# A recurrent attention block and its gated layer on one core: sums of squares by one-column products, an engine chosen per unit, and dummy products

## The chip, the cores and the metric

The kernel runs on one NeuronCore of a Trainium2 chip. The metric is device time in microseconds (us) of one execution: 171.41 us, the median of three runs (170.92 to 173.13).

The core's engines work side by side, each through its own queue in order: TensorE (PE, matrix products; its weight loads, PEld, are a row of their own), VectorE (DVE), ScalarE (ACT), GpSimd (POOL) and SyncE (SP), which in this kernel issues all transfers. SBUF is the working memory, PSUM the memory that products are written to.

## The reference

Four batches of eight heads, 768 steps, head size 48. The first half is a recurrence with a decaying 48x48 state for each head, the second a layer of 384 to 1024 to 384 with a softmax gate and a normalization.

```python
for t in range(S):
    cur = einsum('bhd,bhe->bhde', u * k[t], v[t])
    y[:, :, t] = einsum('bhd,bhde->bhe', r[t], state + cur)
    state = w[t][..., None] * state + einsum('bhd,bhe->bhde', k[t], v[t])
x = y as (B * S, H * D)
h = x @ w_in
e = exp(h - max(h));  solu = h * e / sum(e)
ln = (solu - mean(solu)) / sqrt(var(solu) + 1e-6) * g_ln
out = ln @ w_out
```

All inputs and the output are float32.

## The kernel before, in words

The steps are cut into six chunks of 128 and the batches taken one by one, which makes 24 units (chunk, batch), chunk outermost. A unit's 128 rows pass through some thirty short stages, each a function of its own (lines 213 to 449). The names in the table below, such as `Y7`, are a stage and a unit.

The attention half of a unit: `load` (L110) brings w, k, r and v, 192 KB each. `lw` is the logarithm of w (ACT). `cum` sums it over the chunk by two products with triangular matrices, 384 columns each, and `exp` (ACT) turns the sums into decays in place. `kp` and `rp` (DVE) scale k and r by them, `krk` and `krr` transpose them on PE (four products each, into the PSUM tile `kr_ps`), `kr` (DVE) copies the result out, `M` multiplies them to eight 128x128 score matrices, `m` (ACT) copies those out and `sel` (POOL) sets the part on and below the diagonal of each to zero. The bonus of the current step is `p` = r k, `q` = p u (POOL), `dg` its sum over a head (DVE) and `dv` = v dg (POOL). `Y` (L307) adds on PE, into one PSUM tile `y_ps`: `dv` by a product with the identity, the part from the state, and scores times v (`vb`, v in bf16). `y` (ACT) copies it out. `S`, `et` and `st` (L330 to 371) make the next state: `S` adds the old state (product with the identity), four one-column products that sum the logarithms over the chunk, and k times v; `et` takes the exponential of that sum, `st` multiplies by it in two halves of 64 partitions (DVE).

The layer half: `X` transposes y (PE), `xT` copies it out (DVE), `H` (L388) makes h by 24 products of 128 columns into `h_ps`, `e` (ACT) its exponential, `he` (DVE) h times e. `Oa` and `Ob` (L407) walk over eight slices f of 128 hidden values, four each. For each f there are three products with weights of its own: `he` times the second layer's weights `w2` and a column that gives the mean (385 columns into `o_ps`); `he` times itself, the Gram matrix (128 columns into `g_ps`), of which only the diagonal, the sum of squares, is used; and `e` times a constant column (one column). `junk` (DVE) takes the diagonal, `sq` (ACT), `qm` (POOL) and `lv` (ACT, a logarithm and an exponential) make the scale of each row, and `o` (ACT) scales the output and issues its store.

Once, at the start, `w2` must be built: `gw` scales the eight slices of w_out by the gain (four on DVE, four on ACT), `mean` averages them on PE, `mean_sb` copies that out (ACT), and `w2` (L208) adds it to each slice in eight additions on DVE, in the code's tile names `w`. The first `Oa` needs `w2`. All helpers issue through `InOrder` (L49), which is why most rows of the profile have line 63.

The order of work is a table, `ORDER` (L21): each engine takes its part of the words in the order in which they stand. A load is issued with the word `lw`, four units ahead of it. PSUM is taken from two pools: `big`, two tiles of two banks (`cum`, `M`, `H`), and `small`, four tiles of one bank (the rest). The inputs have six buffers.

## Time and profile before

| | |
|---|---|
| runs | 171.41 us median, 170.92 to 173.13 |
| profiled execution, its own time | 169.39 us |
| its span, first to last instruction | 167.7 us |
| busy PE / DVE / ACT / POOL | 143.0 / 121.2 / 118.0 / 107.5 us |
| bytes moved | 27.09 MB |

A group row of the profile reads: line, engine, operation, what it writes and from what, shape, how often; then busy time in us and the mean of one in ns; then how long the engine idled just before it and for whom. Mean times of neighbours on an engine overlap a little, so that the sum over an engine's groups is larger than its busy time. A row of the timeline begins with its start and its length in us. How fast PE goes is read from the distance between starts, not from the length, since products overlap in its pipeline. The row PEclk of the page, the granted clock, shows nearly full speed throughout.

### The profile page before, as it was taken

What the parts mean: (1) busy time and instruction counts of PE and PEld (TensorE: products, weight loads), DVE (VectorE), ACT (ScalarE), POOL (GpSimd) and SP (SyncE); (2) the same over time, 40 slices, a digit from 0 to 9 for tenths busy, and PEclk for the clock granted to TensorE, in tenths of its full rate; (3) what the DMA queues carried; (4) which work ended last, traced back from release to release, by engine and by line L of the source; (5) the groups of instructions that cost most, each with busy time, mean ns of one, the idle gap of its engine ahead of it and who ended that gap; (6) DMA issues with size and microseconds to landing.
All of it is one profiled execution on the core that took longest, in us unless ns stands there. A gap on an engine that the chain in (4) does not pass through costs nothing.

```text
span 167.7 us, 5377 instructions
## 1 busy us (share of the span) xinstructions
PE 143.0 (85%) x2139; PEld 113.4 (68%) x2139; DVE 121.2 (72%) x280; ACT 118.0 (70%) x243; POOL 107.5 (64%) x157
## 2 busy tenths in 40 slices
PE   0503669928999999999999999999999999999980
PEld 0102336825888888878888778788877878798850
DVE  7008597898978788778988866888677988664430
ACT  3305495618879878788789868987798786767752
...
GB/s 76 224 344 216 348 210 212 170 216 221 177 218 183 218 161 254 188 238 163 240 184 182 266 165 144 185 192 184 192 2 51 0 51 47 51 2 52 92 51 92
DMA packets 104795, 27.09 MB, mean 162 GB/s; under 512 B 100281, under 2 KB 104386, under 8 KB 104770
## 3 DMA queue, kind: packets, MB, share of 16 engines
...
q14 instruction: 9, 0.07, 0.1%
...
## 4 chain that ended last, share of the span: by engine, by line
PE 75%; SPq 8%; DMA 5%; DVE 4%; ACT 2%; POOL 2%; issue 1%; POOLq 0%; DVEq 0%; ACTq 0%
PE o_ps L63 21%; PE h_ps L63 18%; SPq L63 8%; PE y_ps L63 6%; PE g_ps L63 6%; PE kr_ps L63 6%; PE s_ps L63 5%; PE m_ps L63 4%; PE cum_ps L63 4%; DMA wout_f<-in_moe_w_out_dram 3%; DVE w L63 3%; PE x_ps L63 3%; DMA k_in<-in_k_dram 2%; PE mean_ps L63 1%; DVE kr L63 1%
## 5 line engine op out<-in xcount | busy, mean ns | idle before, releaser
L63 PE MATMUL o_ps<-w,he 128*128 128x385 bf16 x192 | 50.7, 325 | 3.4 <-DVE he L63 3.4
L63 PE MATMUL g_ps<-he 128*128 128x128 bf16 x192 | 41.8, 218 | 0.0
L63 POOL TENSOR_SCALAR_AFFINE_SELECT m<-m 128x1024 bf16<-128x1024 bf16 x24 | 26.3, 1096 | 18.3 <-ACT m L63 13.9
L63 PE MATMUL h_ps<-xT,win_sb 128*128 128x128 bf16 x576 | 35.9, 219 | 0.0
L63 PEld LDWEIGHTS <-win_sb 128*128 128x128 bf16 x576 | 32.8, 98 | 0.9 <-DVE xT L63 0.5
L63 PE MATMUL o_ps<-inv_col,e 128*128 128x1 bf16 x192 | 31.9, 166 | 0.0
L63 ACT ACTIVATE e<-h_ps 128x1024 bf16<-128x1024 f32 x24 | 24.5, 1022 | 9.9 <-PE h_ps L63 9.8
L63 DVE TENSOR_TENSOR he<-h_ps,e 128x1024 bf16<-128x1024 f32 x24 | 29.3, 1222 | 2.2 <-ACT e L63 1.3
L63 ACT CAST m<-m_ps 128x1024 bf16<-128x1024 f32 x24 | 24.3, 1012 | 8.5 <-PE m_ps L63 8.2
L63 PEld LDWEIGHTS <-he 128*128 128x128 bf16 x384 | 24.2, 97 | 5.3 <-DVE he L63 3.5
L63 PEld LDWEIGHTS <-e 128*128 128x128 bf16 x192 | 18.5, 96 | 12.8
L63 POOL TENSOR_TENSOR dv<-vb,dg 128x384 bf16<-128x384 bf16 x24 | 19.8, 828 | 9.7 <-DVE dg L63 9.6
L63 POOL TENSOR_TENSOR q<-p,u_bc 128x384 bf16<-128x384 bf16 x24 | 21.8, 911 | 4.6 <-DVE gr L63 4.2
L63 POOL TENSOR_TENSOR p<-r_in,k_in 128x384 bf16<-128x384 f32 x24 | 24.3, 1012 | 0.1
L63 DVE COPY kr<-kr_ps 128x1024 bf16<-128x1024 bf16 x24 | 16.6, 690 | 10.0 <-PE kr_ps L63 9.8
L63 ACT ACTIVATE cum_ps<-cum_ps 128x768 f32<-128x768 f32 x24 | 19.2, 801 | 5.4 <-PE cum_ps L63 3.0
L63 ACT ACTIVATE lw<-w_in 128x384 bf16<-128x384 f32 x23 | 12.0, 522 | 6.7 <-DMA w_in<-in_w_dram 6.7
L63 DVE TENSOR_TENSOR kp<-cum_ps,k_in 128x384 bf16<-128x384 f32 x24 | 13.3, 555 | 3.4 <-ACT cum_ps L63 2.8
L63 PEld LDWEIGHTS <-kr 64*128 64x128 bf16 (+1 forms) x272 | 11.3, 98 | 6.3 <-DVE kr L63 2.8
L63 POOL TENSOR_TENSOR qm<-ss,sq 128x1 f32<-128x1 f32 x24 | 4.5, 190 | 16.9 <-DVE junk L63 13.7
L63 DVE TENSOR_TENSOR st<-s_ps,et 64x192 bf16<-64x192 f32 x40 | 14.1, 353 | 1.6 <-ACT et L63 0.6
L63 ACT ACTIVATE o<-o_ps,rs 128x384 f32<-128x384 f32 x24 | 13.9, 578 | 0.3
...
## 6 DMA issues: line engine op xcount, KB each, us to landing
w_in<-in_w_dram SPq DMA_DIRECT2D x24, 192.0 KB, 4.2
k_in<-in_k_dram SPq DMA_DIRECT2D x24, 192.0 KB, 3.7
r_in<-in_r_dram SPq DMA_DIRECT2D x24, 192.0 KB, 3.9
v_in<-in_v_dram SPq DMA_DIRECT2D x24, 192.0 KB, 4.2
out_dram<-o SPq DMA_DIRECT2D x24, 192.0 KB, 2.7
...
u_row<-in_u_dram SPq DMA_DIRECT2D x1, 1.5 KB
```

Of the source, the lines that this page charges most:

```text
L63: made = make(*args, **kwargs)
```

## The change

The sum of squares no longer comes from the Gram matrix. `hq` squares `he` on ACT or DVE, and `Ob` ends with eight one-column products of `hq` with a column of ones, which write beside the mean in `o_ps`; `g_ps` is gone. `qm` now copies the three sums out and makes the variance in two small instructions, all on DVE; `sq` and `junk` are gone. The four one-column products of the logarithms move from `S` into `cum`, so that `exp` takes the state's decay too; `et` becomes a small multiplication on DVE, and `st` one multiplication over 128 partitions.

The table now names an engine behind a word: `a` ACT, `v` DVE, `g` POOL. So `kr`, `xT`, `m`, `y`, `o`, `hq`, `p`, `q`, `vb`, `dv`, `gw` and the eight additions of `w2` (`wt`) go to different engines in different units. Where `m` is on DVE, one multiplication with the triangular matrix copies and masks, and there is no `sel`. Where `y` is on DVE, it adds `dv` while it copies, and `Y` leaves its product with `dv` out; `Y` with an `x` keeps it. The counts are: `kr` 16 DVE, 8 ACT; `xT` 14 DVE, 10 ACT; `m` 6 DVE, 18 ACT; `y` 14 DVE, 10 ACT; `o` 14 DVE, 10 ACT; `hq` 3 DVE, 21 ACT; `gw` 2 DVE, 3 ACT, 3 POOL; `wt` 4 DVE, 4 POOL; `p` and `vb` one each on DVE, `dv` two, the others POOL. 24 dummy products `dm` of 512 columns on zeros are put in, 19 of them before the first `Oa`, five at the end. The whole order is a new table. The loads of unit 1 now come before the weights, and w_in comes in three pieces.

The diff, cut to its core:

```diff
 ORDER = """
-lw0 cum0 vb0 p0 win1 rows ubc exp0 q0 kp0 p1 rp0 lw1 cum1 dg0 win2 win0 exp1 kp1 krk1 krk0 rp1 krr0 kr0 gw3 M0 dv0 krr1 q1 kr1 m0 dg1 M1 sel0 m1 gw0
...
+dm10 p1g lw0 dm13 dm7 dm12 dm0 p0v dm3 cum0 dm21 exp0 dm20 kp0 et0 krk0 rows rp0 lw1 krr0 cum1 vb0v kr0v M0 ubc exp1 et1 kp1 dm14 m0a q0g krk1 rp1
+sel0 dg0 dv0v krr1 kr1a M1 q1g Y0x win0v y0a dm23 m1v dm5 dm16 win1g X0 win2a gw3a xT0v dg1 H0 vb1g e0 gw2g dv1v Y1 S1 gw0v gw1g y1v gw4a S0 st1 X1
...
+    load(0)
...
-    sp.dma_start(out=win_f, in_=moe_w_in.rearrange("(ko ki) f -> ki ko f", ki=128))
-    load(1)
+    win_v = moe_w_in.rearrange("(ko ki) f -> ki ko f", ki=128)
...
+    load(1)
+    load_w_in(0)
+    load_w_in(1)
+    load_w_in(2)
+    load_w_out(0)
+    load_w_out(1)
+    load(2)
+    for i in range(3, 5):
...
+    own = consts.tile([C, HP, 2], F32)
+    nc.vector.memset(own, 0.0)
+    for a in range(2):
+        nc.vector.memset(own[64 * a:64 * a + 64, :, a:a + 1], 1.0)
+    warm = consts.tile([C, 512], BF16)
+    nc.vector.memset(warm, 0.0)
     inv_col = consts.tile([C, 1], BF16)
-    nc.vector.memset(inv_col, 1.0 / RDF)
...
+    def warm_up(i):
+        w_ps = small.tile([C, 512], F32, tag="s", name="w_ps")
+        pe.matmul(w_ps, lhsT=uti_neg, rhs=warm, start=True, stop=True)
...
-    def setup_w2():
-        for f in range(KF):
-            dve.tensor_add(out=w2[:, f, :DM], in0=gw[:, f, :], in1=mean_sb)
...
+    def setup_w2(f, engine):
+        engine.tensor_add(out=w2[:, f, :DM], in0=gw[:, f, :], in1=mean_sb)
...
     def cumulate(i):
         L = live[i]
         lw = L["lw"]
-        cum = big.tile([C, 2, 512], F32, tag="b", name="cum_ps")
-        pe.matmul(cum[:, 0, :DM], lhsT=uti_neg, rhs=lw[:, :, :D], start=True, stop=True)
-        pe.matmul(cum[:, 1, :DM], lhsT=uts, rhs=lw[:, :, :D], start=True, stop=True)
+        cum = big.tile([C, 1024], F32, tag="b", name="cum_ps")
+        last = units[i][0] == NC - 1
+        pe.matmul(cum[:, 128:512], lhsT=uti_neg, rhs=lw[:, :, :D], start=True, stop=last, skip_group_check=True)
+        pe.matmul(cum[:, 512:896], lhsT=uts, rhs=lw[:, :, :D], start=True, stop=True)
+        if not last:
+            for hp in range(HP):
+                pe.matmul(cum[:, 124 + hp:125 + hp], lhsT=lw[:, 2 * hp:2 * hp + 2, :].rearrange("t a d -> t (a d)"),
+                          rhs=one_col, start=False, stop=(hp == HP - 1), skip_group_check=True)
         L["ex"] = cum
 
     def decays(i):
         cum = live[i]["ex"]
-        act.activation(out=cum[:, :, :DM], in_=cum[:, :, :DM], func=EXP)
+        part = slice(128 if units[i][0] == NC - 1 else 124, 896)
+        act.activation(out=cum[:, part], in_=cum[:, part], func=EXP)
+
+
+    def whole_decay(i):
+        L = live[i]
+        L["et"] = wk.tile([C, HP, 2], F32, tag="et", name="et", bufs=10)
+        dve.tensor_mul(out=L["et"], in0=L["ex"][:, 124:128].unsqueeze(2).to_broadcast([C, HP, 2]), in1=own)
...
-    def transposed_copy(i):
+    def transposed_copy(i, engine):
         L = live[i]
         kr_ps = L["kr_ps"]
         kr = wk.tile([C, 2 * HP, C], BF16, tag="kr", name="kr")
-        dve.tensor_copy(out=kr, in_=kr_ps)
+        copy(engine, kr, kr_ps)
...
-    def scores_copy(i):
+    def scores_copy(i, engine):
         L = live[i]
         m_ps = L["m_ps"]
         m = wk.tile([C, 2, HP, C], BF16, tag="m", name="m")
-        act.copy(out=m, in_=m_ps)
+        if engine is act:
+            act.copy(out=m, in_=m_ps)
+        else:
+            dve.tensor_mul(out=m.rearrange("s a p t -> s (a p) t"), in0=m_ps.rearrange("s a p t -> s (a p) t"),
+                           in1=uts.unsqueeze(1).to_broadcast([C, H, C]))
...
+    def attend(i, with_bonus):
         L = live[i]
         c, b = units[i]
         m, kr, vb, st = L["m"], L["kr"], L["vb"], st_t[b]
         y_ps = small.tile([C, DM], F32, tag="s", name="y_ps")
-        pe.matmul(y_ps, lhsT=ident, rhs=L["dv"].rearrange("t h d -> t (h d)"), start=True, stop=False,
-                         skip_group_check=True)
+        first = True
+        if with_bonus:
+            pe.matmul(y_ps, lhsT=ident, rhs=L["dv"].rearrange("t h d -> t (h d)"), start=True, stop=False,
+                      skip_group_check=True)
+            first = False
         if c > 0:
             for hp in range(HP):
                 pe.matmul(y_ps[:, hp * 2 * D:(hp + 1) * 2 * D], lhsT=kr[:, HP + hp, :], rhs=st[:, hp, :],
-                                 start=False, stop=False, skip_group_check=True)
+                          start=first, stop=False, skip_group_check=True)
+                first = False
         for h in range(H):
             pe.matmul(y_ps[:, h * D:(h + 1) * D], lhsT=m[:, h % 2, h // 2, :], rhs=vb[:, h, :],
-                             start=False, stop=(h == H - 1), skip_group_check=True)
+                      start=first, stop=(h == H - 1), skip_group_check=True)
+            first = False
         L["y_ps"] = y_ps
...
+    def y_copy(i, engine):
         L = live[i]
         y_ps = L["y_ps"]
         y = wk.tile([C, DM], BF16, tag="y", name="y")
-        act.copy(out=y, in_=y_ps)
+        if engine is act:
+            act.copy(out=y, in_=y_ps)
+        else:
+            dve.tensor_add(out=y, in0=y_ps, in1=L["dv"].rearrange("t h d -> t (h d)"))
         L["y"] = y
...
-    def state_decay(i):
-        L = live[i]
-        if units[i][0] == NC - 1:
-            return
-        L["et"] = wk.tile([C, HP], F32, tag="et", name="et")
-        act.activation(out=L["et"], in_=L["s_ps"][:, DM:], func=EXP)
 
     def state_update(i):
         L = live[i]
         c, b = units[i]
         if c == NC - 1:
             return
-        st, s_ps, et = st_t[b], L["s_ps"], L["et"]
-        sv = s_ps[:, :DM].rearrange("p (a e) -> p a e", a=HP)
-        for a in range(2):
-            rows = slice(64 * a, 64 * a + 64)
-            cols = slice(a * D, (a + 1) * D)
-            dve.tensor_mul(out=st[rows, :, cols], in0=sv[rows, :, cols],
-                                 in1=et[rows].unsqueeze(2).to_broadcast([64, HP, D]))
+
+        dve.tensor_mul(out=st_t[b].rearrange("p q (a e) -> p (q a) e", a=2),
+                       in0=L["s_ps"].rearrange("p (h e) -> p h e", h=H),
+                       in1=L["et"].rearrange("p q a -> p (q a)").unsqueeze(2).to_broadcast([C, H, D]))
...
+    def hidden_square(i, engine):
+        L = live[i]
+        L["hq"] = wk.tile([128, KF, C], BF16, tag="hq", name="hq", bufs=3)
+        if engine is act:
+            act.activation(out=L["hq"], in_=L["he"], func=SQUARE)
+        else:
+            dve.tensor_mul(out=L["hq"], in0=L["he"], in1=L["he"])
+
+
     def output(i, part):
         L = live[i]
         e, he = L["e"], L["he"]
         if part == 0:
-            L["o_ps"] = small.tile([C, DM + 2], F32, tag="s", name="o_ps")
-            L["g_ps"] = small.tile([C, C], F32, tag="s", name="g_ps")
-        o_ps, g_ps = L["o_ps"], L["g_ps"]
+            L["o_ps"] = small.tile([C, DM + 3], F32, tag="s", name="o_ps")
+        o_ps = L["o_ps"]
         for f in range(part * KF // 2, (part + 1) * KF // 2):
             pe.matmul(o_ps[:, :DM + 1], lhsT=he[:, f, :], rhs=w2[:, f, :], start=(f == 0), stop=False,
-                             skip_group_check=True)
-            pe.matmul(g_ps, lhsT=he[:, f, :], rhs=he[:, f, :], start=(f == 0), stop=(f == KF - 1))
-            pe.matmul(o_ps[:, DM + 1:], lhsT=e[:, f, :], rhs=inv_col, start=False, stop=(f == KF - 1),
-                             skip_group_check=True)
-
-    def squares(i):
-        L = live[i]
-        junk = wk.tile([C, C], BF16, tag="junk", name="junk")
-        L["ss"] = wk.tile([C, 1], F32, tag="ss", name="ss")
-        dve.scalar_tensor_tensor(out=junk, in0=L["g_ps"], scalar=1.0, in1=ident, op0=MULT, op1=MULT, accum_out=L["ss"])
-
-    def sums(i):
-        L = live[i]
-        L["sq"] = wk.tile([C, 2], F32, tag="sq", name="sq")
-        act.activation(out=L["sq"], in_=L["o_ps"][:, DM:], func=SQUARE)
-
-    def centre(i):
-        L = live[i]
-        L["qm"] = wk.tile([C, 1], F32, tag="qm", name="qm")
-        pool.tensor_sub(out=L["qm"], in0=L["ss"], in1=L["sq"][:, 0:1])
+                      skip_group_check=True)
+            pe.matmul(o_ps[:, DM + 1:DM + 2], lhsT=e[:, f, :], rhs=inv_col, start=False, stop=False,
+                      skip_group_check=True)
+        if part == 1:
+            for f in range(KF):
+                pe.matmul(o_ps[:, DM + 2:], lhsT=L["hq"][:, f, :], rhs=one_col, start=False, stop=(f == KF - 1),
+                          skip_group_check=True)
+
+
+    def variance(i):
+        L = live[i]
+        sums = L["sums"] = wk.tile([C, 3], F32, tag="sums", name="sums")
+        dve.tensor_copy(out=sums, in_=L["o_ps"][:, DM:])
+        neg = wk.tile([C, 1], F32, tag="neg", name="neg")
+        dve.scalar_tensor_tensor(out=neg, in0=sums[:, 0:1], scalar=sums[:, 0:1], in1=sums[:, 2:3], op0=MULT,
+                                 op1=ALU.subtract)
+        L["var"] = wk.tile([C, 1], F32, tag="var", name="var")
+        dve.scalar_tensor_tensor(out=L["var"], in0=sums[:, 1:2], scalar=sums[:, 1:2], in1=neg, op0=MULT,
+                                 op1=ALU.subtract)
...
-        act.activation(out=lv, in_=L["sq"][:, 1:2], func=LN, scale=1e-6 * DF * DF, bias=L["qm"])
+        act.activation(out=lv, in_=L["var"], func=LN)
...
-    def store(i):
+    def store(i, engine):
         L = live[i]
         c, b = units[i]
         o = io.tile([C, DM], F32, tag="o", name="o")
-        act.activation(out=o, in_=L["o_ps"][:, :DM], func=COPY, scale=L["rs"])
+        if engine is act:
+            act.activation(out=o, in_=L["o_ps"][:, :DM], func=COPY, scale=L["rs"])
+        else:
+            dve.tensor_scalar(out=o, in0=L["o_ps"][:, :DM], scalar1=L["rs"], scalar2=None, op0=MULT)
         sp.dma_start(out=out[b * S + c * C:b * S + (c + 1) * C, :], in_=o)
...
+        name, i, choice = re.fullmatch(r"([A-Za-z_]+)(\d*):?([a-z]?)", word).groups()
+        args = [engines[choice]] if choice in engines else []
...
+        if name == "Y":
+            args = [choice == "x"]
+        stages[name](i, *args)
 
```

Three places show how instructions move. The first is PE at the end of a unit's output products (`he`, `e`, `hq` are the weights loaded, `w_192` and `w_204` are the tile `w2`). Before, one of eight rounds:

```order
L63 LDWEIGHTS he
L63 MATMUL o_ps<-w_192,he 128x385
L63 LDWEIGHTS he
L63 MATMUL g_ps<-he 128x128
L63 LDWEIGHTS e
L63 MATMUL o_ps<-inv_col,e 128x1
```

And now, the last of eight rounds and the first of the eight new products behind it:

```order
L67 LDWEIGHTS he
L67 MATMUL o_ps<-w_204,he 128x385
L67 LDWEIGHTS e
L67 MATMUL o_ps<-inv_col,e 128x1
L67 LDWEIGHTS hq
L67 MATMUL o_ps<-one_col,hq 128x1
```

The product of 128 columns has left each round, and eight rows of one column stand behind the eighth.

The second is DVE where `w2` is built and the first h e is made (`he`, unit 0, then unit 1). Before:

```order
L63 TENSOR_TENSOR kp_150<-cum_ps,k_in 128x8x48
L63 TENSOR_TENSOR rp_156<-cum_ps,r_in 128x8x48
L63 TENSOR_TENSOR w_192<-gw,mean_sb 128x384 x8
L63 TENSOR_TENSOR he<-h_ps,e 128x1024
L63 COPY kr<-kr_ps 128x1024
L63 TENSOR_TENSOR st_183<-s_ps,et 64x4x48 x2
```

And now:

```order
L67 TENSOR_TENSOR he<-h_ps,e 128x1024
L67 TENSOR_TENSOR st_195<-s_ps,et 128x384
L67 TENSOR_TENSOR kp_157<-cum_ps,k_in 128x8x48
L67 TENSOR_TENSOR et<-cum_ps,own 128x8
L67 TENSOR_TENSOR rp_165<-cum_ps,r_in 128x8x48
L67 TENSOR_TENSOR w_204<-gw,mean_sb 128x384 x2
L67 TENSOR_REDUCE dg<-q 128x8
L67 TENSOR_TENSOR w_204<-gw,mean_sb 128x384
```

The first `he` now stands ahead of the additions, and DVE makes three of them here and a fourth later; POOL makes the other four.

The third is SP's queue at the start. Before, from the second unit's loads on, with the weights around them:

```order
L63 DMA win_f<-in_moe_w_in_dram 128x3x1024
L63 DMA w_in<-in_w_dram 128x8x48
L63 DMA k_in<-in_k_dram 128x8x48
L63 DMA r_in<-in_r_dram 128x8x48
L63 DMA v_in<-in_v_dram 128x8x48
L63 DMA wout_f<-in_moe_w_out_dram 128x4x384 x2
```

And now:

```order
L67 DMA w_in<-in_w_dram 128x8x48
L67 DMA k_in<-in_k_dram 128x8x48
L67 DMA r_in<-in_r_dram 128x8x48
L67 DMA v_in<-in_v_dram 128x8x48
L67 DMA win_f<-in_moe_w_in_dram 128x1024 x3
L67 DMA wout_f<-in_moe_w_out_dram 128x4x384 x2
```

The weights of the first layer have moved behind unit 1; what follows, the loads of units 2 to 4, stands behind the same bytes as before.

144 lines of the change are left out of this document (72 added, 72 removed).

## The prediction

> **What bounds the kernel now.** I read the busy shares first, then the span in stretches, then the waits, then the timeline of PE.
>
> ```profile
> PE 143.0 (85%) x2139; PEld 113.4 (68%) x2139; DVE 121.2 (72%) x280; ACT 118.0 (70%) x243; POOL 107.5 (64%) x157
> ```
>
> No engine stands out, but the average hides three stages. The stretches are cut at the first and behind the last output product; the columns are length, then busy time of PE, PEld, DVE, ACT and POOL, each with its count, then clock, DMA share and GB/s.
>
> ```profile
> 0.00:30.00 30.00, 14.68 (x116) 8.52 (x117) 16.75 (x58) 13.38 (x21) 14.99 (x28) 1.00 0.93 230
> 30.00:36.50 6.50, 3.17 (x60) 2.93 (x57) 6.34 (x10) 3.04 (x6) 4.24 (x5) 1.00 0.99 195
> 36.50:162.80 126.30, 125.12 (x1967) 102.00 (x1967) 97.84 (x211) 100.31 (x214) 88.06 (x124) 1.00 0.66 147
> 162.80:167.70 4.90, 0.00 (x0) 0.00 (x0) 0.30 (x2) 1.25 (x4) 0.19 (x1) 0.70 0.21 80
> ```
>
> For 126.3 us PE is busy 125.1 while DVE, ACT and POOL have 22, 21 and 30% to spare. So this stretch is PE's work, and a product taken out shortens it. The first 36.5 us are something else: DVE is full from 30 on, and one wait says for what.
>
> ```profile
> 30.16 5.19 DVE L63 TENSOR_TENSOR w<-gw,mean_sb 128x384 bf16<-128x384 bf16 x8 [0.57 <-ACT mean_sb L63]
> 35.27 1.21 DVE L63 TENSOR_TENSOR he<-h_ps,e 128x1024 bf16<-128x1024 f32 x1
> ...
> 36.54 0.34 PE L63 MATMUL o_ps<-w,he 128*128 128x385 bf16 x1 [3.37 <-DVE he L63]
> ```
>
> The eight additions of `w2` hold DVE for 5.2 us, `he` of unit 0 stands behind them, and PE waits 3.4 us for it. The last 4.9 us are the last unit's scale, copy and store.
>
> **PE's work.** What a product costs is the distance to the next start:
>
> ```profile
> 62.62 0.33 PE L63 MATMUL o_ps<-w,he 128*128 128x385 bf16 x1
> 62.78 0.22 PE L63 MATMUL g_ps<-he 128*128 128x128 bf16 x1
> 62.84 0.17 PE L63 MATMUL o_ps<-inv_col,e 128*128 128x1 bf16 x1
> 62.87 0.32 PE L63 MATMUL s_ps<-st,ident 128*128 128x384 bf16 x1
> 63.03 0.24 PE L63 MATMUL s_ps<-one_col,lw 128*128 128x1 bf16 x4
> 63.13 0.33 PE L63 MATMUL s_ps<-vb,kp 128*128 128x96 bf16 x4
> ...
> 65.40 0.33 PE L63 MATMUL y_ps<-dv,ident 128*128 128x384 bf16 x1
> 65.56 0.33 PE L63 MATMUL y_ps<-st,kr 128*128 128x96 bf16 x4
> 65.73 0.36 PE L63 MATMUL y_ps<-vb,m 128*128 128x48 bf16 x8
> 65.93 0.32 PE L63 MATMUL o_ps<-w,he 128*128 128x385 bf16 x1
> ```
>
> A Gram product takes 0.055 us (0.06 as printed), 192 of them 10.6. A one-column product with weights of its own takes 0.025 (four in 0.10 from 63.03); eight narrow ones in a row, each with its own weights, also 0.025 (0.20 from 65.73), so eight weight loads in a row are covered. The 192 new ones cost 192 x 0.026 = 5.0. If their loads were not covered, the price would be that of the Gram products, 10.6, and the swap would bring nothing: the other end. I take 5.0, a gain of **5.6**. The product with `dv`, 0.16, goes in 14 units: **2.2**. The products of the logarithms only move. Together **7.8 us** less for PE, nearly all of it behind the first output product: 126.3 - 7.8 = **118.5**.
>
> **What the others take over.** The nearest rows:
>
> ```profile
> L63 DVE TENSOR_TENSOR he<-h_ps,e 128x1024 bf16<-128x1024 f32 x24 | 29.3, 1222 | 2.2 <-ACT e L63 1.3
> L63 ACT CAST m<-m_ps 128x1024 bf16<-128x1024 f32 x24 | 24.3, 1012 | 8.5 <-PE m_ps L63 8.2
> L63 ACT CAST win_sb<-win_f 128x1024 bf16<-128x1024 f32 x1 | 1.0, 1029 | 0.0
> L63 DVE COPY kr<-kr_ps 128x1024 bf16<-128x1024 bf16 x24 | 16.6, 690 | 10.0 <-PE kr_ps L63 9.8
> L63 DVE TENSOR_TENSOR kp<-cum_ps,k_in 128x384 bf16<-128x384 f32 x24 | 13.3, 555 | 3.4 <-ACT cum_ps L63 2.8
> L63 DVE TENSOR_TENSOR st<-s_ps,et 64x192 bf16<-64x192 f32 x40 | 14.1, 353 | 1.6 <-ACT et L63 0.6
> L63 ACT ACTIVATE o<-o_ps,rs 128x384 f32<-128x384 f32 x24 | 13.9, 578 | 0.3
> L63 ACT CAST y<-y_ps 128x384 bf16<-128x384 f32 x24 | 11.5, 478 | 3.3 <-PE y_ps L63 3.2
> L63 DVE COPY xT<-x_ps 128x384 bf16<-128x384 bf16 x24 | 8.5, 355 | 6.1 <-PE x_ps L63 5.8
> L63 DVE SCALAR_TENSOR_TENSOR junk<-g_ps,ident 128x128 bf16<-128x128 f32 x24 | 6.9, 288 | 8.1 <-PE g_ps L63 4.3 <-PE o_ps L63 3.8
> L63 ACT ACTIVATE sq<-o_ps 128x2 f32<-128x2 f32 x24 | 4.1, 172 | 1.8 <-PE o_ps L63 1.5
> L63 DVE TENSOR_SCALAR gr<-gt_ps 128x8 f32<-128x8 f32 x1 | 0.2, 156 | 0.0
> ```
>
> DVE in the long stretch: 14 `y` and 14 `o` at 0.555 (the `kp` row) +15.5; six `m` at 1.222 +7.3; three `hq` between 0.69 and 1.22, at 0.95, +2.9; 20 `et` at 0.156 +3.1; 20 `st` at 0.555 for 40 at 0.353 -3.0; eight `kr` -5.5; ten `xT` -3.6. The copy of three sums (at most 0.156) and two instructions on one column (between 0 and 0.156 each, say 0.1) stand against `junk`'s 0.288 and its read-out: nothing. Sum +16.7 of row time; neighbours overlap (over all of DVE's groups the means sum to 131 for 121.2 busy), so about nine tenths, **+15**: 97.8 becomes 113, which is 95% of 118.5. ACT: 21 `hq` at 1.029 +21.6, eight `kr` at 1.012 +8.1, ten `xT` at 0.478 +4.8; six `m` -6.1, 14 `y` -6.7, 14 `o` -8.1, 24 `sq` -4.1, 20 `et` at as much as a `sq` -3.4. Sum +6.1, nine tenths +5.5: 100.3 becomes 106, 89%. POOL loses six masks and `qm` and gains little after the start.
>
> So the cover that hid DVE is nearly gone: 28.5 us idle in this stretch before, 5.5 after if PE kept pace. Each queue is in order, and what PE waits for can now stand behind a `y`, an `m` or an `o` of another unit. The added wait lies between 0 (PE keeps pace) and 27 (DVE idles 22.5% as before: 113 / 0.775 = 145.5). In the stretch from 30 to 36.5 DVE was 98% busy, so it can run dense when its operands are there, and `hq` stands several stages of other units' products ahead of the `Ob` that needs it. Behind a late `hq` on ACT wait the next `e` and `m`, and PE's `Ob` and `Y` for those. I take **4**, nearer to the low end.
>
> Transfers do not bind here: 147 GB/s in the long stretch become 147 x 126.3 / 122.5 = 152, and the first 30 us ran at 230. The last 4.9 us keep their length: three small instructions on DVE stand for `junk`, `qm` and `sq`, and the five dummy products at the end have no reader and run beside the last store; should the last store wait for them, five at 0.2 add 1.
>
> **The start.** Of the dummy products, 19 precede the first output product, where PE is busy 17.9 of 36.5 us; at four thirds of 0.16 (512 for 384 columns) they take 4 us, hidden by its idle half; on the path they would cost those 4. In SP's queue unit 1 moves ahead of the weights, past one transfer of 1.5 MB, so that unit 0 and 1 fill PE while the weights land; from unit 2 on nothing arrives sooner. What now decides is the data. The new order puts unit 4's `cum` ahead of the first `Oa`.
>
> ```profile
> 24.66 1.22 SPq L63 DMA_DIRECT2D w_in<-in_w_dram  x1
> ...
> 31.97 0.52 ACT L63 ACTIVATE lw<-w_in 128x384 bf16<-128x384 f32 x1
> ```
>
> ```profile
> w_in<-in_w_dram SPq DMA_DIRECT2D x24, 192.0 KB, 4.2
> ```
>
> Unit 4's w, behind the same bytes as now, is issued at 24.7 and lands 4.2 later, at 28.9; its logarithm takes 0.5, its sums 0.4, `X` 0.2: first `Oa` at 30. On the other side `mean` started at 28.1:
>
> ```profile
> 25.21 0.63 PE L63 MATMUL kr_ps<-ident,kp 128*128 128x128 bf16 x4
> 25.63 0.63 PE L63 MATMUL kr_ps<-ident,rp 128*128 128x128 bf16 x4
> ...
> 28.12 1.48 PE L63 MATMUL mean_ps<-gw,mean_w 128*128 128x384 bf16 x8
> ...
> 32.56 0.38 PE L63 MATMUL kr_ps<-ident,kp 128*128 128x128 bf16 x4
> 32.78 0.39 PE L63 MATMUL kr_ps<-ident,rp 128*128 128x128 bf16 x4
> ```
>
> It now stands earlier on PE, `he` no longer waits for the additions, and half of them go to POOL. I take **30.5** for 36.5, a gain of 6, between 28.9 (w lands) and 36.5 (nothing gained).
>
> The rows also show PE at half rate until about 29: four transposes take 0.42 at 25.21 and 0.22 at 32.56, though the granted clock reads 1.00. The Trainium skill (TensorE: Matmul & The Clock Gate, Part 1) says that PE runs at half clock until it has been busy for about 3.4 us; the trace agrees with the halves, and by that rule the dummies would bring the full rate forward. My sum counts nothing for it, since w of unit 4 decides.
>
> **Sum.** 30.5 + 118.5 + 4 + 4.9 = 157.9 us of span for 167.7. The profiled execution's own time lay 1.7 above its span, which gives 159.6, and 2.0 below the median of the runs. I add half of that: **160.5 us**.
>
> **Rivals.**
> *The order absorbs all.* No added wait, first output at 28.9: 28.9 + 118.5 + 4.9 = 152.3, with 2.7 around it 155. For it: 12 us of slack on ACT. Against it: DVE at 95%.
> *Nothing gained at the start.* The additions interfere:
>
> ```profile
> L63 DVE TENSOR_TENSOR w<-gw,mean_sb x8: 345/668/1155, 30.2 to 35.0; 128x384 bf16<-128x384 bf16 x8
> ```
>
> One took 0.35 to 1.16 us while POOL was at work for most of that time. If DVE and POOL exclude each other there, the split ones come one after the other, four at 0.35 and four at about 0.9 us (POOL's `q` below, of the same size), 5 us, as long as now. First output at 36.5 again: 163.9, with 2.7 around it **166.5**. The Trainium skill (SBUF — State Buffer, Who interferes with whom) says that a DVE instruction with two SBUF inputs and a GpSimd one that reads SBUF lock each other out, which is this case. The spread in the row agrees. Against the rival: the first half of the output needs only four of the eight.
>
> ```profile
> 31.77 0.91 POOL L63 TENSOR_TENSOR q<-p,u_bc 128x384 bf16<-128x384 bf16 x1
> ```
>
> *DVE becomes the bound.* It idles as large a share as before: 30.5 + 145.5 + 4.9 = 180.9, with 2.7 around it **183.5**, slower. It turns when the added wait passes 13.8 us, that is when DVE idles more than 19 us of the stretch. For it: DVE at 95%, in order, with work of five stages more. Against it: DVE's waits before were for PE, which ran dense.
>
> **How the numbers follow.** The forecast 0.54, the order absorbing all 0.20, nothing gained at the start 0.13, DVE as the bound 0.13. Range **151 to 169**: from the second case less 4, to the third and the near half of the fourth. Faster by over 2% (below 168.0; 2% is about what a measurement of this kernel can tell from no change) holds for nearly all of the first three and a little of the fourth, 0.83; within 2% 0.10; slower 0.07.
>
> **What would show it.** Eight `hq` products in about 0.2 us; first `Oa` near 30.5; last output product near 153; DVE over 90% busy between. Wrong if `hq` products take 0.055 each, if the first `Oa` stays at 36, or if PE's waits between come to more than 8 us: then the list of waits names DVE as what they wait for.

## The result and the profile after

The changed kernel takes **161.66 us** (median of four runs, 160.24 to 163.06) against 171.25 for the kernel before on the same chip (four runs, 170.92 to 173.13): a ratio of **0.939**, 95% interval 0.929 to 0.950. Its profiled execution took 161.92 us, with a span of 160.1. Some executions run in a slower state (one of the wide ones below took 230.5 us): medians are over all executions, ratios over those outside that state.

The busy line of the page, then the span in stretches, cut at the first output product, at 112 us, where the last load has just been issued (at 110.7), and behind the last output product. The columns are those of the prediction's table of stretches.

```profile
PE 141.7 (89%) x2147; PEld 109.2 (68%) x2149; DVE 142.9 (89%) x327; ACT 123.4 (77%) x203; POOL 102.5 (64%) x130
```

```profile
0.00:29.10 29.10, 22.31 (x200) 13.46 (x203) 22.91 (x75) 16.86 (x24) 18.05 (x29) 0.82 0.97 240
...
29.10:112.00 82.90, 76.20 (x1258) 61.37 (x1257) 79.46 (x168) 70.22 (x120) 64.42 (x79) 1.00 0.99 208
112.00:155.30 43.30, 41.95 (x690) 33.93 (x689) 38.82 (x81) 35.54 (x58) 20.08 (x24) 1.00 0.17 53
```

The same cut of the kernel before, whose last load is issued at 114.7 us:

```profile
36.50:112.00 75.50, 74.68 (x1186) 61.15 (x1187) 62.46 (x136) 61.56 (x132) 61.35 (x85) 1.00 0.95 199
112.00:162.80 50.80, 50.43 (x784) 40.85 (x780) 35.38 (x76) 38.74 (x83) 26.70 (x40) 1.00 0.24 70
```

Three things are to be seen. The first output product starts at 29.1 instead of 36.5, 7.4 us sooner. From there to the end of the last output product it takes 126.2 us, as long as before: PE's work in it fell from 125.1 to 118.2 us, and its idle time rose from 1.1 to 8.0. And of these 8.0 us, 6.7 lie ahead of 112 us, where the DMA engines are busy 99% of the time and DVE 96%; behind it PE idles 1.4 us of 43. So **the whole net gain was made at the start**, and the 7 us saved in products were given back as waits while loads ran.

The timeline of PE shows the first output product, eight of the new products, and the end:

```profile
29.12 0.33 PE L67 MATMUL o_ps<-w,he 128*128 128x385 bf16 x1
...
33.30 0.34 PE L67 MATMUL o_ps<-one_col,hq 128*128 128x1 bf16 x8
33.50 0.32 PE L67 MATMUL o_ps<-w,he 128*128 128x385 bf16 x1
...
155.12 0.34 PE L67 MATMUL o_ps<-one_col,hq 128*128 128x1 bf16 x8
155.32 0.38 PE L67 MATMUL w_ps<-warm,uti_neg 128*128 128x512 bf16 x1
```

Eight one-column products take 0.20 us, from 33.30 to 33.50. What PE waited for over the whole span (total, times, longest):

```profile
PE kr_ps L67 <- DVE kp L67: 2.2, 3, 1.2
PE w_ps L64 <- POOL uti_neg L152: 1.5, 1, 1.5
PE m_ps L67 <- DVE kr L67: 1.4, 1, 1.4
PE kr_ps L67 <- DVE rp L67: 1.3, 1, 1.3
PE h_ps L67 <- DVE xT L67: 1.2, 2, 0.8
```

The second row and parts of the first and the last belong to the start. The rest are waits for DVE, each short; no single one explains 8 us. Inside the stretch the list has waits of 7.5 us, 6.4 of them for DVE. The groups of DVE show one thing that the prediction had not priced, the two variance instructions on one column:

```profile
L67 DVE SCALAR_TENSOR_TENSOR var<-sums,neg 128x1 f32<-128x1 f32 x24 | 10.6, 441 | 0.8
L67 DVE SCALAR_TENSOR_TENSOR neg<-sums 128x1 f32<-128x1 f32 x24 | 8.8, 367 | 0.8
L67 DVE COPY sums<-o_ps 128x3 f32<-128x3 f32 x24 | 3.6, 152 | 1.8 <-PE o_ps L67 1.7
```

The copy of three columns takes 0.15 us, an instruction on one column two to three times as long. The timeline shows what such a long one stands beside:

```profile
80.23 0.28 DVE L67 SCALAR_TENSOR_TENSOR neg<-sums 128x1 f32<-128x1 f32 x1
...
80.46 0.91 POOL L67 TENSOR_TENSOR q<-p,u_bc 128x384 bf16<-128x384 bf16 x1
80.55 0.84 DVE L67 SCALAR_TENSOR_TENSOR var<-sums,neg 128x1 f32<-128x1 f32 x1
```

`var` started 0.09 us behind POOL's `q` and ended with it. And the list of waits names the loads on POOL and ACT:

```profile
POOL p L67 <- DMA r_in<-in_r_dram: 7.6, 4, 4.7
```

```profile
ACT lw L67 <- DMA w_in<-in_w_dram: 4.2, 5, 1.8
```

This gives the theories. *Lock*: the variance instructions read two operands from SBUF and are shut out while POOL is at work, which costs DVE 9 us. *Loads* (D in the expectations): the transfers hold back the stretch up to 112 us. *PE* (P): PE's products set the time and the waits are incidental. Beside them stands the question which part of the change brought the 7.4 us at the start.

### The profile page after: what moved, and what is told of

It is laid out like the page before. It is cut to its first block, busy times and chain, and to the rows that moved or that the text cites. A ratio compares the mean times of both kernels' runs of the same rounds, so it can differ in the third digit from the quotient of the medians.

```text
span 160.1 us, 5330 instructions
## 1 busy us (share of the span) xinstructions
PE 141.7 (89%) x2147; PEld 109.2 (68%) x2149; DVE 142.9 (89%) x327; ACT 123.4 (77%) x203; POOL 102.5 (64%) x130
## 4 chain that ended last, share of the span: by engine, by line
PE 32%; DVE 31%; SPq 16%; ACT 6%; DMA 6%; issue 6%; DVEq 0%
SPq L67 16%; PE h_ps L67 12%; PE o_ps L67 9%; DVE he L67 7%; DMA w_in<-in_w_dram 5%; DVE neg L67 4%; ACT e L67 3%; DVE var L67 3%; DVE kp L67 3%; PE kr_ps L67 2%; DVE o L67 2%; PE y_ps L67 2%; PE m_ps L67 2%; DVE rp L67 2%; PE s_ps L67 2%
## 5 line engine op out<-in xcount | busy, mean ns | idle before, releaser
L67 PE MATMUL o_ps<-w,he 128*128 128x385 bf16 x192 | 42.7, 325 | 0.5 <-DVE xT L67 0.3
L67 POOL TENSOR_SCALAR_AFFINE_SELECT m<-m 128x1024 bf16<-128x1024 bf16 x18 | 19.6, 1091 | 19.6 <-ACT m L67 19.5
L67 PEld LDWEIGHTS <-he 128*128 128x128 bf16 x192 | 18.5, 97 | 10.7 <-DVE he L67 0.4
L67 ACT ACTIVATE hq<-he 128x1024 bf16<-128x1024 bf16 x21 | 22.1, 1052 | 0.0
L67 ACT ACTIVATE cum_ps<-cum_ps 128x772 f32<-128x772 f32 (+1 forms) x24 | 19.1, 798 | 3.2 <-PE cum_ps L67 2.2
L67 POOL TENSOR_TENSOR dv<-vb,dg 128x384 bf16<-128x384 bf16 x22 | 18.5, 847 | 3.6 <-DVE dg L67 2.6
L67 ACT CAST m<-m_ps 128x1024 bf16<-128x1024 f32 x18 | 18.2, 1010 | 1.2 <-PE m_ps L67 1.0
L67 PEld LDWEIGHTS <-e 128*128 128x128 bf16 x192 | 18.5, 96 | 0.5 <-issue 0.4
L67 PEld LDWEIGHTS <-kp 128*128 128x128 bf16 x176 | 11.2, 98 | 5.5 <-DVE kp L67 3.8
L67 ACT ACTIVATE lv<-var 128x1 f32<-128x1 f32 x24 | 4.9, 203 | 11.4 <-DVE var L67 11.2
L67 PE MATMUL m_ps<-kr 64*128 64x128 bf16 x192 | 10.0, 225 | 4.1 <-DVE kr L67 1.4
L67 DVE TENSOR_REDUCE dg<-q 128x8 f32<-128x384 bf16 x24 | 13.0, 542 | 0.3 <-POOL q L67 0.3
```

The costliest lines, as they stand in the source:

```text
L67: made = make(*args, **kwargs)
```

## The experiments

One table first. "First" is the start of the first output product, "stretch" from there to the end of the last output product (to within 0.2 us), with PE's busy and idle time in it, all from the profiled execution; the ratio is to the kernel before, run beside each on the same chip.

| kernel | median us | ratio, interval | first | stretch | PE busy | PE idle |
|---|---|---|---|---|---|---|
| before | 171.25 | 1 | 36.5 | 126.2 | 125.1 | 1.1 |
| changed | 161.66 | 0.939 (0.929 to 0.950) | 29.1 | 126.2 | 118.2 | 8.0 |
| wide ones | 166.58 | 0.961 (0.951 to 0.972) | 29.8 | 129.6 | 124.1 | 5.5 |
| sums from PSUM | 160.36 | 0.932 (0.924 to 0.940) | 29.4 | 125.1 | 117.2 | 7.9 |
| stores late | 160.64 | 0.933 (0.931 to 0.935) | 29.5 | 125.0 | 117.7 | 7.3 |
| both | **154.63** | **0.899 (0.895 to 0.903)** | 29.9 | 118.3 | 116.7 | 1.6 |
| loads as before | 166.42 | 0.969 (0.967 to 0.971) | 33.8 | 125.7 | 117.7 | 8.0 |
| `w2` all on DVE | 164.17 | 0.958 (0.950 to 0.966) | 30.1 | 125.4 | 117.5 | 7.9 |
| no dummies | 163.07 | 0.946 (0.938 to 0.955) | 29.4 | 125.8 | 117.9 | 8.0 |
| engines as before | 178.29 | 1.038 (1.035 to 1.042) | 33.8 | 137.3 | 122.4 | 15.0 |
| `y` on ACT | 166.85 | 0.971 (0.965 to 0.977) | 29.1 | 131.0 | 120.4 | 10.6 |
| masks on POOL | 167.52 | 0.975 (0.968 to 0.983) | 30.6 | 129.6 | 120.5 | 9.0 |
| copies as before | 168.32 | 0.979 (0.972 to 0.985) | 30.3 | 132.3 | 119.8 | 12.5 |
| both, `y` on DVE | 158.53 | 0.921 (0.914 to 0.927) | 29.6 | 122.5 | 118.0 | 4.5 |

### What paces the stretch

**Wide ones.** The new products multiply by 120 columns of ones, not one; only the first of the 120 results is used.

```diff
-                pe.matmul(o_ps[:, DM + 2:], lhsT=L["hq"][:, f, :], rhs=one_col, ...
+                pe.matmul(o_ps[:, DM + 2:], lhsT=L["hq"][:, f, :], rhs=ones, ...
```

> The 192 products of squares are taken with 120 columns of ones instead of one column; the first of the equal columns is used. TensorE gets 192 times about 0.027 us more, 5.2 us, and no other engine anything. If TensorE sets the pace of the long stretch, the time rises by 4 to 5 us, to 166; if VectorE does, TensorE's gaps take it up and the time rises by less than 2 us. Half of it would say that both do by turns.

The group of the wide products, to be held against 8.1 us for the narrow ones:

```profile
L67 PE MATMUL o_ps<-ones,hq 128*128 128x120 bf16 x192 | 13.9, 216 | 0.0
```

PE is busy 5.9 us longer in the stretch, and the stretch grows by 3.4, since PE idles 2.5 less; the time grows by 2.2% of the time before, some 4 us. That looks as if PE's work counted in part, but the time is not lost where the products are. Eight wide ones take 0.41 us (37.72 to 38.13) for 0.20, in every unit. By the starts of `e` on ACT, however, the run lies 4.2 us behind the changed kernel at the fourth unit, 4.1 at the 15th and 3.6 at the last. The early loss goes with PE's clock, which the trace shows at 0.50 from 28.5 to 31.9 and from 42.2 to 45.6 us; the changed kernel has 1.00 throughout the stretch. The block of `H` in the second spell, which takes 1.50 us at full rate:

```profile
43.06 2.71 PE L67 MATMUL h_ps<-xT,win_sb 128*128 128x128 bf16 x24
```

So this run does not show PE pacing the part with the loads: there the wider products slip under waits that are there anyway. Behind the loads, from the 16th unit to the last, the time between the `e` grows from 37.9 to 38.6 us, by 0.8 for some 1.7 of added products. POOL's wait for `r_in` falls from 7.6 to 3.4 us.

**Sums from PSUM.** The second operand of the two variance instructions comes from the PSUM tile itself.

```diff
-  ...(out=neg, in0=sums[:, 0:1], scalar=sums[:, 0:1], in1=sums[:, 2:3], op0=MULT,
+  ...(out=neg, in0=sums[:, 0:1], scalar=sums[:, 0:1], in1=L["o_ps"][:, DM + 2:DM + 3], op0=MULT,
...
-  ...(out=L["var"], in0=sums[:, 1:2], scalar=sums[:, 1:2], in1=neg, op0=MULT,
+  ...(out=L["var"], in0=L["o_ps"][:, DM + 1:DM + 2], scalar=sums[:, 1:2], in1=neg, op0=MULT,
```

> The two small instructions that make the variance take the third sum and the second sum from PSUM, so that neither has two inputs in SBUF. In the changed kernel they take 0.22 us when POOL is idle and up to 1.1 us when it works, 19.4 us in all. Theory A (they wait for POOL's instruction, and VectorE's fullness makes TensorE wait): each takes 0.22 to 0.26 us, never over 0.3; VectorE's busy time falls by 8 to 9 us, from 142.9 to 134; TensorE's 8 us of gaps in the long stretch shrink and the time falls by 2 to 5 us, to 157 to 160. Theory B (they are slow because each needs the result of the one before): their mean stays near 0.40 us and the time at 161.7. Theory C (they wait for POOL, but TensorE alone sets the time): the rows shrink as in A and the time moves by less than 1 us.

The durations of the two (minimum, median, maximum in ns), of the changed kernel and then of this one:

```profile
L67 DVE SCALAR_TENSOR_TENSOR neg<-sums x24: 219/221/1093, 34.2 to 155.7; 128x1 f32<-128x1 f32 x24
...
L67 DVE SCALAR_TENSOR_TENSOR var<-sums,neg x24: 218/220/1111, 34.5 to 155.9; 128x1 f32<-128x1 f32 x24
```

```profile
L67 DVE SCALAR_TENSOR_TENSOR neg<-sums,o_ps x24: 214/216/217, 34.6 to 154.9; 128x1 f32<-128x1 f32 x24
...
L67 DVE SCALAR_TENSOR_TENSOR var<-o_ps,sums,neg x24: 217/219/220, 34.8 to 155.1; 128x1 f32<-128x1 f32 x24
```

The median stays at 0.22 us, and the long ones are gone: with one operand in PSUM none takes more than 0.22, where 1.1 occurred. This is the lock, and it had cost DVE 19.4 us less 48 x 0.218, 8.9 us. The Trainium skill (SBUF — State Buffer, Who interferes with whom) says that only the port pair that DVE and GpSimd share causes contention, "and it's an exclusive lock"; the two rows agree.

But the time fell by about 1 us, not by nine (theory A asked for 2 to 5, theory C for less than 1), and the interval overlaps that of the changed kernel. What DVE gains is lost to the loads, twice. By the starts of `e`, the run is 1.9 us ahead at the eighth unit and 0.6 behind at the ninth, where ACT waits for a load:

```profile
67.92 0.53 ACT L67 ACTIVATE lw<-w_in 128x384 bf16<-128x384 f32 x1 [2.46 <-DMA w_in<-in_w_dram]
68.35 1.01 ACT L67 ACTIVATE e<-h_ps 128x1024 bf16<-128x1024 f32 x1
```

At the 13th it is 1.1 ahead again, and then that is gone too. POOL's timeline at that place, of the changed kernel and of this one:

```profile
95.36 0.83 POOL L67 TENSOR_TENSOR dv<-vb,dg 128x384 bf16<-128x384 bf16 x1
100.86 1.95 POOL L67 TENSOR_TENSOR p<-r_in,k_in 128x384 bf16<-128x384 f32 x2 [4.66 <-DMA r_in<-in_r_dram]
```

```profile
94.34 0.83 POOL L67 TENSOR_TENSOR dv<-vb,dg 128x384 bf16<-128x384 bf16 x1
100.91 1.96 POOL L67 TENSOR_TENSOR p<-r_in,k_in 128x384 bf16<-128x384 f32 x2 [5.74 <-DMA r_in<-in_r_dram]
```

The `dv` ahead comes 1.0 us sooner, the `p` behind it at the same time: the load lands when it lands.

**Stores late.** The last load is issued at 110.7 us, and a dozen stores stand among the loads in SP's queue. Here they wait until the last load has been issued.

```diff
-        o = io.tile([C, DM], F32, tag="o", name="o")
+        o = spare.pop(0) if spare else io.tile([C, DM], F32, tag="o", name="o")
...
-        sp.dma_start(out=out[...], in_=o)
+        late.append((out[...], o))
+        if loaded == NU:
+            flush()
...
+    spare = [wout_f[:, f, :] for f in range(KF)] + [win_o[:, f * DM:(f + 1) * DM] for f in range(KF)]
```

> The changed kernel with one difference: no output is stored until the last load has been issued; the first sixteen outputs wait in the memory of the two weight inputs, which is read out by then. The same bytes move. Theory D: the stream of loads paces part of the stretch, and the dozen stores that stand among the loads (1.2 us of queue for two of them at 111.6 us in the changed kernel's trace) hold it up by 6 to 10 us: the last load is issued at 101 to 106 us instead of 113, POOL's p waits for r_in in all under 2 us instead of 7.6, ACT's lw for w_in under 1 us instead of 4.2, and the time falls by 1 to 3 us, 158.5 to 160.5. Rival F (loads come as their buffers come free, the stores only fill gaps): last load still after 109 us, the waits stay, time within 1 us of 161.7. Against both: if the stores that are left bunch up behind the last load, the end comes later and the time rises.

The last load is issued at 107.9 instead of 110.7, which is between what the two theories said, and POOL waits 3.2 us for `r_in`, none of it longer than 1.2; the time falls by about 1 us. Up to the last unit's w the loads are issued 6 to 7 us sooner (that w at 101.6 for 108.0), but then SP waits 4.3 us, until 106.8, for a buffer that DVE's `kp` frees: with the loads early, DVE holds them up. Taken alone this run does not decide. Whether the stores cost the loads their share of the DMA engines or their place in SP's queue, no run separates.

**Both.** The two edits together.

> The changed kernel with the third and second sum read from PSUM (as in the run of that name) and with the stores held back until the last load is issued. Theory D: the first alone gave 1.2 us because the waits moved to the loads (5.7 us for r_in, 4.2 us for w_in); with the loads early too, DVE's 9 us less of work can be used: 155 to 158, faster than either edit alone by at least 2 us. Rival G (PE paces all that is left: 110 us of products in the stretch of 118.5, and its waits are for data of its own unit): 159.5 to 161, as with the PSUM inputs alone.

This one decides. Its stretches, cut where its own last load has been issued (105.1), and the end of its output products:

```profile
29.90:106.00 76.10, 74.77 (x1254) 60.98 (x1253) 72.62 (x167) 69.65 (x119) 63.42 (x78) 1.00 0.98 194
106.00:148.20 42.20, 41.95 (x694) 34.05 (x692) 37.78 (x82) 35.68 (x58) 20.96 (x25) 1.00 0.34 113
```

```profile
148.02 0.34 PE L67 MATMUL o_ps<-one_col,hq 128*128 128x1 bf16 x8
```

Each edit alone brought 1.1 to 1.2 us of the stretch, both bring **7.9**: 118.3 us, of which PE idles 1.6. DVE and the loads were two limits of nearly the same length side by side, and taking away either left the other. The starts of `e` on ACT, per unit, tell it by place: between the 13th and the 16th of the 24 lie 16.1 us in the changed kernel, 17.7 with the sums from PSUM, 14.7 with the stores late, 13.6 with both; between the 16th and the last, with the loads all but over, 37.9, 36.5, 37.9 and 36.5. Behind the loads the PSUM edit is worth its 1.4 us alone; among them it needs the other.

This version beats both kernels: 0.899 of the time before, 0.895 to 0.903.

### What brought the early start

**Loads as before.** Unit 1 is loaded behind w_in, which comes in one piece, and unit 0 behind two small rows, as before.

```diff
-    load(0)
...
+    load(0)
...
+    sp.dma_start(out=win_f, in_=win_v)
...
-    load_w_in(0)
-    load_w_in(1)
-    load_w_in(2)
```

> The changed kernel with the loads at the start in the order of before: unit 0, the input weights in one piece, unit 1, then the output weights. Theory S (the order of loads at the start gave the early start: the changed kernel's first output product comes at 29.1 us, the one of before at 36.5): unit 1's stages come about 5 us later (1.5 MB at 300 GB/s), PE's first 20 us hold less work, which has to be done later: time up by 2 to 5 us, 163.5 to 167, first output product at 30 to 34. Rival T (unit 4's w decides the first output product, and the weights stand ahead of it in both orders): first output product within 0.7 us of 29.1 and the time within 1.5 us of 161.7.

The first output product, and the wait of PE that has grown (0.2 us between 8 and 34 us in the changed kernel):

```profile
33.76 0.33 PE L67 MATMUL o_ps<-w,he 128*128 128x385 bf16 x1
```

```profile
PE cum_ps L67 <- ACT lw L67: 4.8, 2, 4.6
```

`lw` of unit 4 starts at 32.1 us here and waits for no load. The first output product is 4.6 us later, the stretch 0.5 shorter, the time 4.8 higher: of the 7.4 us, **4.6 hang on the order of the first loads**.

**`w2` all on DVE.** The four additions on POOL go back to DVE.

```diff
-... wt5g dg2 wt0v m2v dm11 e1 dv2g wt2g hq0a ... Oa1 wt6g kp3 wt4g ...
+... wt5v dg2 wt0v m2v dm11 e1 dv2g wt2v hq0a ... Oa1 wt6v kp3 wt4v ...
```

> All eight additions that build the second layer's weights are on VectorE, at the places in the order where they stand. Theory A (the split brought the first output product forward): four more additions at 0.65 to 0.75 us on VectorE ahead of it, and it starts 1.5 to 3 us later than 29.1; the time rises by as much. Theory B (VectorE and POOL exclude each other there, so that the split saves nothing): the first output product stays within 0.7 us. Theory C (data of unit 4 decide): the same as B, but the second layer's weights are ready before the first output product in both kernels.

First output product 1.0 us later, at 30.1, between what theory A (1.5 to 3) and theory B (0.7) said. The median is higher by more than that (0.958 for 0.939), while the profiled execution, at 162.12, was 0.2 above that of the changed kernel. In it the starts of `e` lie 1.6 us behind at the 15th unit and 0.2 from the 16th on, so the later start was taken up before the loads ended; why the other executions are slower no profile shows, and it stays open. The additions themselves (ns, as above), here and in the changed kernel:

```profile
L67 DVE TENSOR_TENSOR w<-gw,mean_sb x8: 340/670/1065, 23.4 to 33.3; 128x384 bf16<-128x384 bf16 x8
```

```profile
L67 DVE TENSOR_TENSOR w<-gw,mean_sb x4: 592/666/1068, 23.5 to 31.6; 128x384 bf16<-128x384 bf16 x4
L67 POOL TENSOR_TENSOR w<-gw,mean_sb x4: 904/909/1027, 24.8 to 29.4; 128x384 bf16<-128x384 bf16 x4
```

They spread over 8 to 10 us in both, with other work between them, where the kernel before did all eight in 5.2 us in a row ahead of `he`. By these rows the new order, more than the split, took them off the path.

**No dummies.** All 24 dummy products are left out.

```diff
-dm10 p1g lw0 dm13 dm7 dm12 dm0 p0v dm3 cum0 ...
+p1g lw0 p0v cum0 ...
```

> All 24 dummy products are left out, nothing else. Theory A (they bring TensorE's full rate forward from about 29 to 18.5 us): without them the products of the start, the first hidden layers and the mean above all, run at half rate again, the first output product starts 1 to 2 us later than 29.1, at 30 to 31, and the time rises by 1 to 2 us. Theory B (the data of unit 4 decide the first output product): half rate is back, but the first output product stays within 0.5 us and the time within 0.5 us. Theory C (they are in the way): the time falls by up to 1 us.

First output product at 29.4 (+0.3), ratio 0.7% higher, with overlapping intervals: no effect that can be told from none. The timeline of PE shows why little was to be had. The two blocks of 24 products of `H` ahead of the first output product, in the changed kernel and without dummies:

```profile
16.28 2.51 PE L67 MATMUL h_ps<-xT,win_sb 128*128 128x128 bf16 x24 [0.45 <-DVE xT L67]
...
23.80 1.50 PE L67 MATMUL h_ps<-xT,win_sb 128*128 128x128 bf16 x24
```

```profile
16.58 2.72 PE L67 MATMUL h_ps<-xT,win_sb 128*128 128x128 bf16 x24 [0.45 <-DVE xT L67]
...
24.19 1.50 PE L67 MATMUL h_ps<-xT,win_sb 128*128 128x128 bf16 x24
```

The first block is slow and the second at full rate in both. PE reaches its full rate between the two, with or without dummies. The clock readings in the traces say when: at 18.4 us with them (after a first spell from 4.8 to 8.2) and 19.8 without, at 17.2 to 18.5 in the runs with sums from PSUM, `w2` on DVE and stores late, and at 21.4 in the one with both, which all have the dummies. In the kernel before it was 28.2. So it was not the dummies that brought the lasting full rate forward, as theory A had it; it came with the rest of the new start.

### What the engine choice is worth

**Engines as before.** `kr` and `xT` on DVE, `m`, `y` and `o` on ACT, all masks on POOL, and `Y` with its `dv` product in all units; squares, sums, decays, order and dummies stay.

```diff
-... kr1a M1 q1g Y0x win0v y0a dm23 m1v dm5 ...
+... kr1v M1 q1g Y0x win0v y0a dm23 m1a sel1 dm5 ...
```

> The changed kernel with the engine choices of the kernel before for all units: copies kr and xT on DVE, m, y and o on ACT, the mask on POOL for all units and the dv product of Y on PE in all 24 (14 more). Squares, one-column products, state decays, the order and the dummies stay. By rows of the changed kernel DVE loses 14 us (23.5 of m, y, o against 8.9 of kr, xT), ACT gains 8 (20.7 against 12.9), POOL gains 6.5, PE gains 2.2. Theory P (PE paces): 2 to 4 us more, 163.5 to 166, PE's busy time 144, DVE's waits longer by more than 10 us. Rival Q (the choice itself balances the engines, ACT at 131 us becomes what PE waits for): 168 to 174, with PE's waits on ACT's rows m, y, e over 8 us. Rival R (DVE was the bound): faster than the changed kernel, below 160.

178.3 us, slower than all three theories said, and slower than the kernel before. No engine is full; its page and two groups of DVE (at the end of a row: idle time just before, and for whom):

```profile
PE 147.6 (84%) x2163; PEld 111.3 (63%) x2163; DVE 128.9 (73%) x311; ACT 128.2 (73%) x219; POOL 108.8 (62%) x136
```

```profile
L67 DVE TENSOR_TENSOR he<-h_ps,e 128x1024 bf16<-128x1024 f32 x24 | 29.3, 1220 | 9.1 <-ACT e L67 9.0
...
L67 DVE COPY xT<-x_ps 128x384 bf16<-128x384 bf16 x24 | 8.4, 350 | 9.3 <-PE x_ps L67 9.3
```

DVE has 14 us less to do, ACT 5 more, and now DVE idles 18 us for ACT and PE in these two rows alone (1.6 and 1.0 in the changed kernel), while PE idles 15.0 us of the stretch. They wait for one another in turn. To see which choice matters, three runs undo one each.

**`y` on ACT**, with 14 more `dv` products.

```diff
-... Y1 S1 gw0v gw1g y1v ...
+... Y1x S1 gw0v gw1g y1a ...
```

> The changed kernel with one of the three engine choices undone: Y takes its dv product on PE in all 24 units (14 more) and y is read out on ACT in all (14 moved from DVE). The run with all three choices undone had a span 15.7 us longer: first output product 4.7 later, stretch between first and last output product 7.7 longer, tail 3.5 longer. Theory H (the three parts add up, each by its own place): here PE gets 14 products more, 2 to 5 us, and PE sets the stretch: 164 to 167. Rival I (no part costs by itself, they fill each other's gaps; only ACT with all of y, o and m is too much): under 163.5.

**Masks on POOL**, six of them, with `m` on ACT.

```diff
-... y0a dm23 m1v dm5 ...
+... y0a dm23 m1a sel1 dm5 ...
```

> The changed kernel with the second choice undone: the six masked products that DVE read out and masked in 1.21 us (units 1, 2, 4, 7, 15, 18) are read out on ACT and masked on POOL, about 2.1 us one behind the other. Theory H: two of them stand in the first 25 us, and the first output product comes 3 to 5 us later, as it did with all three choices undone (33.8); POOL's queue (p, q of later units) stands behind the masks; 164 to 167. Rival I: first output product at 29 to 30, time under 163.5.

**Copies as before**: `kr`, `xT` on DVE, `o` on ACT.

```diff
-... krr1 kr1a M1 ... xT1a rp2 ... kp7 o2v e4 ...
+... krr1 kr1v M1 ... xT1v rp2 ... kp7 o2a e4 ...
```

> The changed kernel with the third choice undone: kr and xT copied on DVE in all units (8 and 10 moved from ACT), o on ACT in all (14 moved from DVE). DVE's busy time stays (8.9 for 8.5), ACT's falls by 4.9. Theory H: the tail gets 2 to 3.5 us longer, since the last eight o are read out by ACT behind its lv and rs, and the order was made for the other engines: 163.5 to 166. Rival I: under 163.5, since ACT, with 123 us, has less to do.

In ratios to the time before they cost 3.2, 3.6 and 4.0%, in us 5.4, 6.1 and 6.8; the sum, 18.3, is near the 17.0 (9.9%) of all three at once. So they add up, as theory H said, though masks and copies come out above its ranges, and not at the places that it named. For `y`, PE's busy time in the stretch grows by 2.2 us, which is 14 x 0.16, and its idle time by 2.6. For the masks, the first output product comes only 1.5 later; PE's busy time in the stretch grows by 2.3 us with the same products, of which some 1.7 are, by estimate, half of a spell of 3.4 us at half clock (0.50 from 42.8 to 46.2 us; the block of `H` in it takes 2.77 us). For the copies, the tail keeps its length; the stretch grows by 6.1, of which 4.5 is idle time of PE, though DVE's own work in it is 2 us less than in the changed kernel, and the granted clock is 0.50 until 32.3 us. The waits of PE that grew, with `y` on ACT (0.3 for `y` on DVE in the changed kernel) and then with the copies as before (1.4 and 1.2):

```profile
PE x_ps L67 <- ACT y L67: 2.9, 3, 1.2
```

```profile
PE m_ps L67 <- DVE kr L67: 4.1, 3, 2.0
PE h_ps L67 <- DVE xT L67: 4.0, 5, 1.4
```

In these two the copy that PE needs next stands in its engine's queue behind other units' work; for the masks no single wait grew as much. By these rows the place in the queue counts, and not the sum of busy times alone. No run writes a new order for the old engines to test it: the order of the table stayed as it was written for the new choices, so these runs price the choices within that order and not at their best.

**Both, `y` on DVE.** To the best version, nine more `Y` without their `dv` product.

```diff
-... Y3x exp5 ... krk5 y3a p6g ...
+... Y3 exp5 ... krk5 y3v p6g ...
```

> The kernel with both edits (PSUM inputs, stores held back; 154.6 us, chain of waits 69% PE) and the dv product taken off PE in nine more units, whose y DVE reads out with the addition (9 times 0.55). PE loses nine products of 384 columns, 1.5 to 3 us; ACT loses 4.3, DVE gets 5, 140 us of some 151. Theory P2 (with the lock and the stores out of the way PE sets the time): 151.5 to 153.5. Rival V (DVE with 140 us is too full again): 154.6 or more, PE's waits for DVE rows above their 5 us.

158.5 us, 3.9 worse. In the stretch PE's busy time rose by 1.3 us, though nine products are gone, and its idle time by 2.9. It now waits for `y` on DVE:

```profile
PE x_ps L67 <- DVE y L67: 2.3, 3, 1.1
```

Its waits for rows of DVE add to 7.2 us, 4.4 in the run with both. So far rival V was right: there is room on PE's list but none left in DVE's queue. But that is not all of the 3.9 us. By the starts of `e`, 2.6 of them arise at the fourth unit, where PE waits for `y` and then runs at half clock (0.50 from 39.4 to 42.8 us, by estimate half of it lost, 1.7):

```profile
39.34 0.46 PE L67 MATMUL x_ps<-ident,y 128*128 128x128 bf16 x3 [1.11 <-DVE y L67]
...
40.66 2.54 PE L67 MATMUL h_ps<-xT,win_sb 128*128 128x128 bf16 x24
```

Whether that spell comes in every execution one trace cannot tell.

## Why the prediction came out as it did

The median, 161.7, is 1.2 above the forecast of 160.5, and the direction held. The bound named (PE, with DVE nearly full) held only behind the loads; up to 112 us DVE and the loads set the pace. The two halves of the gain were forecast as 6.0 at the start and 3.8 in the stretch, and came as 7.4 and 0.0: that the sum came so near is in part luck, since one error took back some of the other. One of the three signs of being wrong was reached: PE idles 8.0 us in the stretch, for a limit of 8, and its list there names DVE. The last output product came at 155.3 us, not near 153.

- **The products**: right. Eight `hq` in 0.20 us; PE's work in the stretch fell by 7.0 us for 7.8.
- **The added wait**, 4 us: mis-sized, it was 6.9. That it need not have been there, the low end of the bounds given, the run with both edits shows: its stretch of 118.3 us is near the 118.5 of the sum, with an added wait of 0.5.
- **The variance on DVE**, "say 0.1" for each of two instructions on one column: the step that failed first. An instruction on one column takes 0.22 us even undisturbed, and with the lock 0.37 and 0.44 on average, which makes 19.4 us for 4.8. Inside the stretch these two and the copy of the sums take 22.5 us of row time where `junk` and its read-out took 8.5: 14 us that the sum put at nothing. The prediction had the lock before its eyes, in the row of the `w2` additions, and applied it there alone; the variance instructions, with two SBUF operands beside a busy POOL, stood under it too. DVE was busy 118.3 us in the stretch instead of 113, and no more than that only because other terms were counted too high: of the 14 `y`, 14 `o` and six `m`, 12, 12 and four fall into the stretch. ACT's 106 was right (105.8).
- **"Transfers do not bind here"**: wrong, and the reason is an average. 147 GB/s was the mean of a stretch in which loads run only to 115 us; the cut at 112 shows 199 GB/s at a DMA share of 0.95 even before the change, and 208 at 0.99 after. The 230 GB/s of the first 30 us, held up as spare, were with the large weight transfers among them. In the run with both edits, where PE keeps its pace, the last load is issued at 105.1 us, some ten sooner than before; in the changed kernel it was 110.7.
- **The first output product**, 30.5: it came at 29.1. The chain was as described: `lw` of unit 4 at 27.7, `X` at 28.9, then the first `Oa`. But that unit 4's w decides was true only because unit 1 came early: with the loads as before the same order started at 33.8, and `lw` of unit 4 then waited for no load. The prediction gave this part no price of its own; it is the largest single one. The split of the additions is worth 1.0 there; the dummies, which the sum had at nothing, 0.3 at most; the masks and copies undone move it by 1.5 and 1.2.
- **The tail**, 4.9: 4.8. **Own time beside span**, 1.7: 1.8.
- **The rivals.** "Nothing gained at the start" fell. "The order absorbs all" (155) is nearly what both edits give, 154.6. "DVE becomes the bound" asked for an idle share of DVE as before; that is what the choices as before produce (21% idle in the stretch, 178 us), not because DVE is full but because the queues wait for each other.
